# Weight decoding in one run of 24 steps, and the bias laid into the mixing's bank by ScalarE

## The chip, the core and the metric

The kernel runs on one core of a Trainium2 chip. Five engines work side by side, each through its own list of instructions in order: TensorE (PE; its weight loads are shown apart as PEld) multiplies matrices into PSUM banks, VectorE (DVE) and ScalarE (ACT) do elementwise work, GpSimd (POOL) does almost nothing here, and SyncE (SP) issues every DMA of the kernel. An instruction that needs another engine's result waits on a semaphore, and everything behind it on its engine waits too. The metric is device time in microseconds, the median of several runs. Before the change it is 1982.3 us (3 runs, 1982.04 to 1982.46).

## The reference, cut to what matters

```python
X = np.fft.rfft(x, axis=1)                      # x: 4 x 3072 x 256, along 3072
Yr = Xr @ w_r - Xi @ w_i + b_r                  # the mixing, 256 x 256
Yi = Xr @ w_i + Xi @ w_r + b_i
Yr = np.sign(Yr) * np.maximum(np.abs(Yr) - lam, 0.0)   # the same for Yi
x = np.fft.irfft(Yr + 1j * Yi, n=3072, axis=1)
h = x @ w_in;  g = h * np.tanh(softplus(h));  x = g @ w_out          # 256 -> 2048 -> 256
xk = mu_k * x + (1 - mu_k) * x_prev;  xr = mu_r * x + (1 - mu_r) * x_prev
k = np.maximum(xk @ w_k, 0);  out = sigmoid(xr @ w_r2) * (k * k @ w_v)   # 256 -> 1024 -> 256
```

All arrays are float32 but the weights of the last two layers, which the kernel reads as 64-bit words (`raw`, two int32 each) and decodes on the chip: float64 to a pair of float32r numbers, a high and a low part. Every product with such a pair is three matmuls.

## The kernel before

The kernel has two parts. `part1` does the two Fourier transforms with the mixing between them, `part2` the rest. Part 1 takes about 325 us, part 2 the other 1650 us, in which nothing is changed.

Part 1 splits the transform of 3072 into 24 x 128. The 24-point stage is additions on DVE (`f1_ops` forward, on a batch in a tile `a`; `f3_ops` inverse, on a tile `g`), the 128-point stage is matmuls. It runs 48 steps, u = 0 to 47: four batches (b) of 12 frequency groups (t, with `NT = 12`). For each u there are three pieces of PE work: F(u) (`emit_F`, eight records into a bank `xps`), M(u) (`emit_M`, the mixing into a bank `yps`, 12 matmuls and a 13th for the bias), I(u) (`emit_I`, into `bps`). Step u issues, in this order on PE, F(u+1), M(u), I(u-1). Between them stand ACT and DVE: `post_F` copies `xps` into `xh` (ACT) and the rest into `xl` (DVE), which M needs; `post_M` and `post_M2` are the shrinking of Y, `yb<-yps` once on ACT and once on DVE, which I needs; `post_I` copies `bps` into `bs` (ACT), which SP writes to DRAM (`b_dr`).

The bias goes in through PE: `pick` (a 128 x 128 selection of rows) times `bias` (b_r and b_i in two rows, as high and low part). In groups with t = 0 M consists of two halves of 256 columns with 13 matmuls each.

The engines' lists are laid down by the loop over u (`manual_schedule`): the text's order is each engine's order. DVE's additions are a background (`Background`) that the loop fills in between by a plan of costs: `bg.until` puts in additions up to a planned time, `bg.flush` all that fall due. `F1_AT` says when the forward additions of the next batch join it, `F3_PART1` when the two halves (h = 0, 1) of batch 0's inverse do; `bg.step` loads such a half (`g<-b_dr`, 1536 KB) as soon as the half before is through the list.

The decoding is a pipeline over pieces (`Weights`): `wq.vec()` lays down one piece's DVE work (`q<-raw` twice, `q<-q,sg`, and a subtraction of the piece two calls older), `wq.sca()` its ACT work (`sg`, `sg`, `q`, and the high part), and asks for the next piece's `raw` (512 KB). There are 25 pieces: 9 of w_k, w_v and w_r (`park_piece`, parked in DRAM as `w_dr`), 8 of w_in (`win_piece`) and 8 of w_out (`wout_piece`). Before the change five parked pieces are decoded in steps 6 to 14, one a step (`NPARK`, `PARK_AT`), and the other twenty in steps 36 to 47, two a step (`dec = 2`). In a step with `dec` the first `wq.vec()` stands ahead of `post_M2(u - 1)` and `post_F(u + 1)` on DVE:

```python
emit_F(u + 1); post_M(u - 1)
if dec: emit(wq.vec())
bg.until(...); post_M2(u - 1)
bg.until(...); post_F(u + 1)
if dec: emit(wq.sca(2))
post_I(u - 2)
if dec == 2: emit(wq.vec()); emit(wq.sca(2))
emit_M(u); emit_I(u - 1)
```

A batch of x is 3 MB in ten DMAs on SP (`new_a`, `load_x`), issued at t = 11 two batches ahead: at u = 11 and at u = 23. All DMAs are on SP's one queue.

Of the kernel before, what the change touches and what calls it, by code (L numbers as in the profile page):

```python
# [10 lines left out]
F32 = mybir.dt.float32  # L11
# [13 lines left out]
NB = 4  # L25
# [4 lines left out]
NT = 12  # L30
# [6 lines left out]
START = (20500, 20500)  # L37
SLACK = (2000, 3200)

NPARK = 5  # L40
PARK_AT = (6, 15)

F3_PART1 = {(1, 4): [(0, 0)], (1, 8): [(0, 1)]}
F3_PART2 = {1: (1, 0), 3: (1, 1), 5: (2, 0), 8: (2, 1), 10: (3, 0), 14: (3, 1)}
# [69 lines left out]
def tile_fft_mix_moe_channel_mix(  # L114
# [26 lines left out]
    def emit(ops):  # L141
        for e in ops:
            e()
# [10 lines left out]
    def mm(o, l, r, start, stop, **kw):  # L154
        T.matmul(out=o, lhsT=l, rhs=r, start=start, stop=stop, **kw)  # L155
# [258 lines left out]
    wt = {}  # L414
# [31 lines left out]
    def decode(raw, parts, scale=1.0):  # L446
        hw, lw = raw[:, :, 1], raw[:, :, 0]
        tl = {}

        def a0():  # L450
            sg = tl["sg"] = pools["st"].tile([128, 512], F32, tag="sg", name="sg")
            return [lambda: act(sg.bitcast(I32), hw.bitcast(F32), ACTF.Copy, scale=14000.0),
                    lambda: act(sg, sg.bitcast(I32), ACTF.Sign)]

        def v0():
            q = tl["q"] = pools["st"].tile([128, 512], F32, tag="q", name="q", bufs=3)
            qi = q.bitcast(I32)
            return [lambda: V.tensor_scalar(out=qi, in0=hw, scalar1=0x08000000, scalar2=3,
                                            op0=ALU.bitwise_xor, op1=ALU.logical_shift_left),
                    lambda: stt(qi, lw, 29, qi, ALU.logical_shift_right, ALU.bitwise_or)]  # L460

        def a1():
            return [lambda: act(tl["q"], tl["q"], ACTF.Abs)]

        def v1():
            return [lambda: stt(tl["q"], tl["q"], 3.4e38, tl["sg"], ALU.min, MULT)]

        def a2():
            tl["p"] = parts(tl["q"])
            return [lambda hi=hi, v=v: act(hi, v, ACTF.Copy, scale=scale) for hi, lo, v in tl["p"]]  # L470

        def v2():
            if scale == 1.0:
                return [lambda hi=hi, lo=lo, v=v: tt(lo, v, hi.bitcast(F32), SUB) for hi, lo, v in tl["p"]]
            return [lambda hi=hi, lo=lo, v=v: stt(lo, v, scale, hi.bitcast(F32), MULT, SUB)
                    for hi, lo, v in tl["p"]]

        return a0, v0, v1, a2, v2, a1

    def win_piece(i):  # L480
        raw = raw_piece(w_in[:, 256 * i:256 * i + 256])
        cs = slice(256 * i, 256 * i + 256)
        w = wt["in"]
        return decode(raw, lambda q: [(w[:, 0, :, cs], w[:, 1, :, cs],
                                q.rearrange("p (k f) -> p k f", k=2))])

    def wout_piece(i):
# [12 lines left out]
    def park_piece(i):  # L500
        raw = raw_piece(parked[i])
        tl = {}

        def parts(q):
            t = tl["t"] = yhl_p.tile([128, 2, 512], F32R, tag="yl", name="wp")
            return [(t[:, 0, :], t[:, 1, :], q)]
        a0, v0, v1, a2, v2, a1 = decode(raw, parts)
        return a0, v0, v1, a2, lambda: v2() + [lambda: nc.sync.dma_start(out=w_dr[i], in_=tl["t"].bitcast(F32))], a1
# [62 lines left out]
    def part1():  # L571
        with ExitStack() as es:
# [11 lines left out]
            fm, im = {}, {}  # L584
            bias = c1.tile([128, 512], F32R, name="bias")
            pick = c1.tile([128, 2, 128], F32R, name="pick")
            zero = c1.tile([128, 64], F32, name="zero")
            As = {}

# [25 lines left out]
            def post_F(u):  # L615
# [7 lines left out]
                if t == 0:  # L623
# [5 lines left out]
                                     in_=zero[:, 0:4].rearrange("p (a o) -> p a o", o=1), func=ACTF.Copy)  # L629
                    xt[u] += (zh, zl)  # L630

            def emit_M(u):
                t = u % NT
                ps = psy.tile([128, 512], F32, tag="y", name="yps")
                xs = xt.pop(u)
                if t:
                    groups = [(slice(0, 512), ((0, 256, 0), (1, 0, 0)))]
                else:

                    groups = [(slice(0, 256), ((0, 256, 0), (1, 0, 2))),  # L640
                              (slice(256, 512), ((0, 512, 2), (1, 256, 0)))]
                for gs, parts in groups:
                    n = gs.stop - gs.start
                    todo = []
                    for zl, lo in ((0, 0), (0, 1), (1, 0)):
                        for h in range(2):
                            w = wt["mix", h][lo]
                            for r, c0, z in parts:
                                todo.append((xs[z + zl][:, h, 128 * r:128 * r + 128], w[:, c0:c0 + n]))
                    todo.append((pick[:, 0 if t else 1, :], bias[:, gs]))  # L650
                    for i, (l, r) in enumerate(todo):
                        mm(ps[:, gs], l, r, i == 0, i == len(todo) - 1)
                yps[u] = ps


            def post_M(u):
                yb = yb_p.tile([128, 512], F32, tag="yb", name="yb")
                act(yb, yps[u], ACTF.Relu, bias=-LAM)
                ybt[u] = yb
# [66 lines left out]
            bg.add(both(z[8:], m[:4]) + m[4:])  # L726
            bg.flush()
            emit_F(0)
            post_F(0)
            bg.add(both(t0[0][1], t0[1][1]) + both(t0[0][2][:10], t0[1][2][:10]), 4)  # L730
            bg.add(both(t0[0][2][10:], t0[1][2][10:]), 8)
# [4 lines left out]
            for u in range(NU):  # L736
                b, t = divmod(u, NT)
                if t == NT - 1 and b + 2 < NB:
                    new_a(b + 2)
                if t == F1_AT[b] and b + 1 < NB:  # L740
                    hs = [f1_ops(As[b + 1], h) for h in range(2)]
                    for i, due in ((slice(14), 0), (slice(14, 24), 4), (slice(24, None), 8)):
                        bg.add(both(*[(h[0] + h[1])[i] for h in hs]), NT * (b + 1) + due)
                bg.jobs += F3_PART1.get((b, t), [])
                bg.step()
                if u == NU - NT - 1:
                    wt["in"] = big.tile([128, 2, 2, 2048], F32R, tag="big", name="win")
                    todo = [lambda: win_piece(0)]
                    for i in range(8):
                        if i < 7:  # L750
                            todo.append(lambda i=i: win_piece(i + 1))
                        todo.append(lambda i=i: wout_piece(i))
                    late = [lambda i=i: park_piece(i) for i in range(NPARK, 9)]
                    wq = Weights(todo[:6] + late + todo[6:])
                    wq.load(3)
                dec = 0
                if b == NB - 1:
                    dec = 2
                elif PARK_AT[0] <= u < PARK_AT[1]:
                    dec = 1  # L760
                    if u == PARK_AT[0]:
                        wq = Weights([lambda i=i: park_piece(i) for i in range(NPARK)])
                        wq.load(2)
                bg.flush(u + 1)
                if u == 6:
                    S.activation(out=mu1, in_=mu, func=ACTF.Copy, scale=-1.0, bias=1.0)
                pe += 1710 * (u + 1 < NU)
                if u + 1 < NU:
                    emit_F(u + 1)
                if u:  # L770
                    post_M(u - 1)
                if dec:
                    emit(wq.vec())
                    bg.clock += 2100
                if u:
                    bg.until(y_at + SLACK[0])
                    post_M2(u - 1)
                    y_at = bg.spend(y_at, 602)
                if u + 1 < NU:
                    bg.until(pe + 700 + SLACK[1])  # L780
                    post_F(u + 1)
                    x_next = bg.spend(pe + 700, 602)
                if dec:
                    emit(wq.sca(2))
                if u > 1:
                    post_I(u - 2)
                if dec == 2:
                    emit(wq.vec())
                    emit(wq.sca(2))
                    bg.clock += 2100  # L790
                emit_M(u)
                pe = max(pe, x_at + 300) + 2770
                y_new = pe + 700
                if u:
                    emit_I(u - 1)
                    pe = max(pe, y_at + 300) + 1710
                x_at, y_at = x_next, y_new
                if b == NB - 1 and t == 10:
                    bg.drain()
                    load_y(0)  # L800
            while wq.busy():
                emit(wq.vec())
                emit(wq.sca(2))
            for h in range(2):
                emit(split_y(0, h)[1])
            post_M(NU - 1)
            post_M2(NU - 1)
            post_I(NU - 2)
            emit_I(NU - 1)
            post_I(NU - 1)  # L810
# [256 lines left out]
```

## Time and profile before

| | |
|---|---|
| median of 3 runs | 1982.3 us (1982.04 to 1982.46) |
| the profiled execution's own time | 1981.86 us |
| its span (first to last instruction) | 1979.9 us |
| PE busy | 1958.0 us, 99% |
| DVE busy | 1141.4 us, 58% |
| ACT busy | 929.0 us, 47% |
| DMA | 106.66 MB, mean 54 GB/s |

The numbers of the trace are from one execution; times in it count from the span's start. An instruction's busy time reaches past the start of the next one on its engine, so what one costs its engine is read from start to start. The chain of waits follows back from the last instruction what released each: what stands in it set the time.

### The profile page before, as it was taken

The numbers are of one execution on the slowest core, as the hardware profiler recorded it, in microseconds if no ns is written. First come the engines' busy times: TensorE is split into PE (matmuls) and PEld (weight loads), VectorE is DVE, ScalarE is ACT, GpSimd is POOL, SyncE is SP. The second block draws the span as 40 slices with busy tenths as digits, with TensorE's granted clock in tenths as the row PEclk, the third lists the DMA queues.
The fourth block names the chain that finished last, engine by engine and source line by source line (L and its number), as shares of the span: only waits on it lengthen the run. The fifth ranks groups of instructions, "written<-read, shape, count | busy, mean of one in ns | idle before, by whom it ended". The sixth has DMA issues, their size and how long they took to land.

```text
span 1979.9 us, 25685 instructions
## 1 busy us (share of the span) xinstructions
PE 1958.0 (99%) x10084; PEld 1686.2 (85%) x10084; DVE 1141.4 (58%) x2183; ACT 929.0 (47%) x1525; POOL 13.2 (1%) x28
## 2 busy tenths in 40 slices
PE   6999999999999999999999999999999999999999
PEld 5888888888888888888888888888888888888888
DVE  8999976665654754465375445555544544444444
ACT  2422286344544554454445444444544544454455
POOL 0000000000000000000000000000000000000000
PEclk9999999999999999999999999999999999999999
DMA  9445276111011010101101001011000000000000
GB/s 279 150 138 170 70 245 200 39 32 65 22 33 54 22 44 11 54 22 33 54 22 54 1 22 54 5 33 38 22 1 22 22 11 12 22 23 1 22 11 22
DMA packets 104554, 106.66 MB, mean 54 GB/s; under 512 B 7017, under 2 KB 85489, under 8 KB 103409
## 3 DMA queue, kind: packets, MB, share of 16 engines
q1 hardware_dynamic: 104432, 105.02, 16.7%
q8 instruction: 79, 1.29, 0.3%
q14 instruction: 43, 0.34, 0.1%
HBM read 62.53 MB, written 42.47 MB: 53 GB/s over the span
## 4 chain that ended last, share of the span: by engine, by line
PE 97%; DMA 1%; DVE 1%; ACT 0%; issue 0%; SPq 0%; DVEq 0%; ACTq 0%
PE a L155 26%; PE hps L155 26%; PE v L155 14%; PE kps L155 13%; PE yps L155 7%; PE bps L155 4%; PE xps L155 4%; PE zps L155 3%; DMA a<-in_x_dram 1%; DMA w_dr<-wp 0%; DVE g L146 0%; ACT sg L152 0%; SPq L266 0%; DVE q L149 0%; ACT q L152 0%
## 5 line engine op out<-in xcount | busy, mean ns | idle before, releaser
L863 DVE CAST gh<-u 128x512 fp32r<-128x512 f32 x384 | 163.2, 425 | 747.5 <-PE a L155 598.2
L155 PE MATMUL a<-gh,wo 128*128 128x512 f32 x1536 | 536.3, 390 | 0.0
L155 PE MATMUL hps<-yh,win 128*128 128x512 f32 x1536 | 534.7, 389 | 0.0
L152 ACT ACTIVATE u<-hps 128x512 f32<-128x512 f32 x384 | 229.7, 598 | 525.0 <-PE hps L155 368.8
L155 PEld LDWEIGHTS hps<-yh,win 128*128 128x128 f32 x1536 | 288.3, 188 | 60.3
L155 PEld LDWEIGHTS a<-gh,wo 128*128 128x128 f32 x1536 | 288.4, 188 | 58.0
L155 PE MATMUL a<-gl,wo 128*128 128x512 f32 x768 | 299.9, 390 | 0.0
L155 PE MATMUL hps<-yl,win 128*128 128x512 f32 x768 | 298.8, 389 | 0.0
L155 PE MATMUL kps<-b,wkt 128*128 128x512 f32 x960 | 280.1, 390 | 0.0
L155 PE MATMUL v<-b,kh 128*128 128x256 f32 x1536 | 275.8, 281 | 0.0
L146 DVE TENSOR_TENSOR gl<-u,gh 128x512 fp32r<-128x512 f32 x384 | 263.6, 687 | 3.6
L155 PEld LDWEIGHTS v<-b,kh 128*128 128x128 f32 x1536 | 243.7, 190 | 7.6
L155 PE MATMUL v<-b,kl 128*128 128x256 f32 x768 | 215.8, 281 | 0.0
L155 PEld LDWEIGHTS kps<-b,wkt 128*128 128x128 f32 x960 | 179.1, 188 | 36.1
L152 ACT ACTIVATE ka<-kps 128x512 f32<-128x512 f32 x192 | 115.0, 599 | 185.5 <-PE kps L155 185.5
L155 PEld LDWEIGHTS hps<-yl,win 128*128 128x128 f32 x768 | 144.1, 188 | 29.9
L155 PEld LDWEIGHTS a<-gl,wo 128*128 128x128 f32 x768 | 144.5, 188 | 26.6
L146 DVE TENSOR_TENSOR kl<-ka,kh 128x512 fp32r<-128x512 f32 x192 | 132.5, 690 | 32.8 <-ACT ka L152 19.1
L155 PEld LDWEIGHTS v<-b,kl 128*128 128x128 f32 x768 | 144.1, 188 | 0.0
L152 ACT ACTIVATE ka<-ka 128x512 f32<-128x512 f32 x192 | 121.4, 632 | 6.3
L152 ACT ACTIVATE kh<-ka 128x512 fp32r<-128x512 f32 x192 | 121.4, 632 | 6.3
L146 DVE TENSOR_TENSOR g<-g 128x128 f32<-128x128 f32 (+3 forms) x272 | 107.5, 433 | 1.2
(80 smaller groups left out, 1926.8 us busy)
## 6 DMA issues: line engine op xcount, KB each, us to landing
b_dr<-bs SPq DMA_DIRECT2D x48, 256.0 KB, 2.2
g<-b_dr SPq DMA_DIRECT2D x8, 1536.0 KB, 6.8
y<-y_dr SPq DMA_DIRECT2D x48, 256.0 KB, 3.2
out_dram<-r SPq DMA_DIRECT2D x48, 256.0 KB, 2.2
y_dr<-g SPq DMA_DIRECT2D x80, 64.0 KB, 1.6
w_dr<-wp SPq DMA_DIRECT2D x9, 512.0 KB, 5.9
a<-in_x_dram SPq DMA_DIRECT2D x8, 512.0 KB, 6.2
y_dr<-g SPq DMA_DIRECT2D x32, 128.0 KB, 1.9
```

The lines of the kernel that those rows point to most:

```text
L146: V.tensor_tensor(out=o, in0=a, in1=b, op=op)
L152: S.activation(out=o, in_=i, func=f, **kw)
L155: T.matmul(out=o, lhsT=l, rhs=r, start=start, stop=stop, **kw)
L863: return [lambda: V.tensor_copy(hi, u), lambda: tt(lo, u, hi.bitcast(F32), SUB)]
```

## The change

It does two things, and three small ones go with them.

The decoding: all 25 pieces are one pipeline, begun at the end of step 23's preparations (`DECODE_FROM = 24`) and run one piece a step in steps 24 to 47, two in steps 38, 41, 43 and 45 (`TWICE`). The nine parked pieces come first. At most two `raw` tiles are asked for ahead, where it was three.

The bias: the two possible bias images (all rows alike; the first row different, for t = 0) are made once by two matmuls `cps<-bias,pick`, and ACT copies them into SBUF (`full`). For u of 3 and more, `pre_M(u)` has ACT copy `full` into the bank `yps`, a step ahead of M(u), and all of M's matmuls add to it (`start` is False). For u below 3 `pre_M` is still a matmul. Of 52 bias matmuls (44 of 512 columns, 8 of 256) five remain, of 512 columns.

Beside these, the plan's cost of M is lowered from 2770 to 2550, the bank `yps` of u+1 is taken in step u rather than in step u+1, and at the end of part 1 the shrinking of the last Y stands ahead of the splitting of part 2's first input on DVE.

```diff
-NPARK = 5
-PARK_AT = (6, 15)
+DECODE_FROM = 24
+TWICE = (38, 41, 43, 45)
...
+            full = [c1.tile([128, 512], F32, name=f"full{i}") for i in range(2)]
...
+            def pre_M(u):
+                ps = yps[u] = psy.tile([128, 512], F32, tag="y", name="yps")
+                i = 0 if u % NT else 1
+                if u < 3:
+                    mm(ps, pick[:, i, :], bias, True, False, skip_group_check=True)
+                else:
+                    act(ps, full[i], ACTF.Copy)
+
             def emit_M(u):
...
-                ps = psy.tile([128, 512], F32, tag="y", name="yps")
+                ps = yps[u]
...
-                    todo.append((pick[:, 0 if t else 1, :], bias[:, gs]))
                     for i, (l, r) in enumerate(todo):
-                        mm(ps[:, gs], l, r, i == 0, i == len(todo) - 1)
-                yps[u] = ps
+                        mm(ps[:, gs], l, r, False, i == len(todo) - 1, skip_group_check=True)
...
             emit_F(0)
+
+            for i in range(2):
+                ps = psb.tile([128, 512], F32, tag="b", name="cps")
+                mm(ps, pick[:, i, :], bias, True, True)
+                act(full[i], ps, ACTF.Copy)
             post_F(0)
...
-                    todo = [lambda: win_piece(0)]
+                if u == DECODE_FROM - 1:
+                    todo = [lambda i=i: park_piece(i) for i in range(9)] + [lambda: win_piece(0)]
...
-                    late = [lambda i=i: park_piece(i) for i in range(NPARK, 9)]
-                    wq = Weights(todo[:6] + late + todo[6:])
-                    wq.load(3)
-                dec = 0
-                if b == NB - 1:
-                    dec = 2
-                elif PARK_AT[0] <= u < PARK_AT[1]:
-                    dec = 1
-                    if u == PARK_AT[0]:
-                        wq = Weights([lambda i=i: park_piece(i) for i in range(NPARK)])
-                        wq.load(2)
+                    wq = Weights(todo)
+                    wq.load(2)
+                dec = 0 if u < DECODE_FROM else 2 if u in TWICE else 1
...
+                if u == 0:
+                    pre_M(0)
+                if u + 1 < NU:
+                    pre_M(u + 1)
...
-                pe = max(pe, x_at + 300) + 2770
+                pe = max(pe, x_at + 300) + 2550
...
+            post_M(NU - 1)
+            post_M2(NU - 1)
             for h in range(2):
                 emit(split_y(0, h)[1])
-            post_M(NU - 1)
-            post_M2(NU - 1)
```

Since the freed steps 6 to 14 let the background run earlier, the change moves work that its lines do not name. The first place is SP's list around the load of the fourth batch of x (`a<-in_x_dram`, step 23). Before, the stores of the first inverse half (`y_dr<-g`) stand behind it:

```order
L266 DMA a<-in_x_dram 128x5x128
L266 DMA a<-in_x_dram 128x8x128
L291 DMA y_dr_70<-g 128x3x128
L291 DMA y_dr_70<-g 128x128
L678 DMA b_dr_58<-bs 128x2x256
L291 DMA y_dr_70<-g 128x2x128
```

and in the changed kernel all sixteen stores of that half stand ahead of the ten pieces of x (the last eleven between two `b_dr` stores directly ahead of x), and behind x the load of the second half and two loads of `raw`:

```order
L266 DMA a<-in_x_dram 128x5x128
L266 DMA a<-in_x_dram 128x8x128
L277 DMA g<-b_dr_57 128x3072
L442 DMA raw<-in_moe_w_k_dram 128x2x512 x2
L685 DMA b_dr_58<-bs 128x2x256
L442 DMA raw<-in_moe_w_k_dram 128x2x512
```

What moved: the stores from behind x to ahead of it, and 1536 KB of `g` and 512 KB for each `raw` to directly behind it. The second place is DVE's list at step 24. Before, yb(23) stands between the additions of the inverse half:

```order
L146 TENSOR_TENSOR xl<-xps,xh 128x512
L146 TENSOR_TENSOR g<-g 128x512
L149 SCALAR_TENSOR_TENSOR yb<-yps,yb 128x512
L149 SCALAR_TENSOR_TENSOR g<-g 128x4x128 x2
L149 SCALAR_TENSOR_TENSOR g<-g 128x512 x2
L149 SCALAR_TENSOR_TENSOR g<-g 128x4x128 x2
L146 TENSOR_TENSOR xl<-xps,xh 128x512
```

and in the changed kernel those additions are through, and the first piece's two instructions stand between xl(24) and yb(23):

```order
L149 SCALAR_TENSOR_TENSOR g<-g 128x4x128 x2
L146 TENSOR_TENSOR xl<-xps,xh 128x512
L149 SCALAR_TENSOR_TENSOR yb<-yps,yb 128x512
L146 TENSOR_TENSOR xl<-xps,xh 128x512
L458 TENSOR_SCALAR q<-raw 128x512
L149 SCALAR_TENSOR_TENSOR q<-raw,q 128x512
L149 SCALAR_TENSOR_TENSOR yb<-yps,yb 128x512
L146 TENSOR_TENSOR xl<-xps,xh 128x512
```

What moved: yb(23) now stands behind an instruction that reads the first `raw`. The third place is DVE's list from one yb to the next where two pieces are decoded. Before (such a step in the last batch; DVE has only the two pieces and `xl`):

```order
L149 SCALAR_TENSOR_TENSOR yb<-yps,yb 128x512
L146 TENSOR_TENSOR xl<-xps,xh 128x512
L146 TENSOR_TENSOR wp<-q,wp 128x512
L149 SCALAR_TENSOR_TENSOR q<-q,sg 128x512
L458 TENSOR_SCALAR q<-raw 128x512
L149 SCALAR_TENSOR_TENSOR q<-raw,q 128x512
L146 TENSOR_TENSOR wp<-q,wp 128x512
L149 SCALAR_TENSOR_TENSOR q<-q,sg 128x512
L458 TENSOR_SCALAR q<-raw 128x512
L149 SCALAR_TENSOR_TENSOR q<-raw,q 128x512
L149 SCALAR_TENSOR_TENSOR yb<-yps,yb 128x512
```

and in the changed kernel, from step 38 to step 39 (the second inverse half's additions on `g` stand there too):

```order
L146 TENSOR_TENSOR g<-g 128x256 x2
L146 TENSOR_TENSOR g<-g 128x128 x7
L146 TENSOR_TENSOR xl<-xps,xh 128x512
L146 TENSOR_TENSOR win<-q,win 128x2x256
L149 SCALAR_TENSOR_TENSOR q<-q,sg 128x512
L458 TENSOR_SCALAR q<-raw 128x512
L149 SCALAR_TENSOR_TENSOR q<-raw,q 128x512
L146 TENSOR_TENSOR wo<-q,wo 128x256 x2
L149 SCALAR_TENSOR_TENSOR q<-q,sg 128x512
L458 TENSOR_SCALAR q<-raw 128x512
L149 SCALAR_TENSOR_TENSOR q<-raw,q 128x512
L149 SCALAR_TENSOR_TENSOR yb<-yps,yb 128x512
```

What moved: additions on `g`, which before were done ahead of the last batch, stand in the same stretch as two pieces.

## Rows read from the trace of the kernel before

**Rows 1.** The page: granted clock by slice, and the chain's shares by engine.

```profile
PEclk9999999999999999999999999999999999999999
...
PE 97%; DMA 1%; DVE 1%; ACT 0%; issue 0%; SPq 0%; DVEq 0%; ACTq 0%
```

**Rows 2.** The longest wait of PE in part 1: us in total, times, longest.

```profile
PE xps L155 <- DVE g L146: 17.6, 2, 16.2
```

**Rows 3.** The chain, in order of time: start, us, records.

```profile
19.19 4.84 PE xps L155 x12
...
35.61 2.96 PE yps L155 x13
...
167.96 0.89 PE xps L155 x8
...
178.38 1.73 PE bps L155 x8
```

**Rows 4.** Timeline of PE, a bias matmul and what follows: start, us.

```profile
108.08 0.39 PE L155 MATMUL yps<-bias,pick 128*128 128x512 f32 x1
108.31 1.90 PE L155 MATMUL bps<-im,yb 128*128 128x256 f32 x8
```

**Rows 5.** Timeline of SP's issues, steps 23 and 24 and the start of step 36.

```profile
164.89 9.18 SPq L266 DMA_DIRECT2D a<-in_x_dram  x10
...
171.69 2.37 SPq L266 DMA_DIRECT2D a<-in_x_dram  x1
...
177.01 7.30 SPq L291 DMA_DIRECT2D y_dr<-g  x14
...
246.01 1.01 SPq L442 DMA_DIRECT2D raw<-in_moe_w_in_dram  x2
```

**Rows 6.** DMAs, us to landing: step 23's last x; w_dr behind x; all w_dr.

```profile
a<-in_x_dram SPq DMA_DIRECT2D x1, 512.0 KB, 7.7
...
w_dr<-wp SPq DMA_DIRECT2D x1, 512.0 KB, 6.5
...
DMA to landing us min/median/max: 2.6/5.9/6.5
```

**Rows 7.** Stretches: us; PE, PEld, DVE, ACT, POOL busy (x); clock; DMA; GB/s.

```profile
187.50:190.50 3.00, 3.00 (x15) 2.52 (x14) 3.00 (x4) 1.09 (x2) 0.00 (x0) 1.00 0.97 348
...
186.00:248.00 62.00, 62.00 (x286) 53.00 (x285) 57.56 (x131) 17.82 (x33) 0.00 (x0) 1.00 0.31 96
248.00:318.00 70.00, 69.74 (x328) 59.78 (x327) 59.24 (x107) 62.09 (x119) 0.00 (x0) 1.00 0.68 220
```

**Rows 8.** The same stretch, DVE's instructions on the decoding's tile q alone.

```profile
248.00:318.00 70.00, 46.61 (x85) 1.00 0.68 220
```

**Rows 9.** Timeline of DVE: a first piece, and a step with two pieces.

```profile
250.13 0.43 DVE L458 TENSOR_SCALAR q<-raw 128x512 int32<-128x512 int32 x1 [3.60 <-DMA raw<-in_moe_w_in_dram]
...
251.20 0.69 DVE L149 SCALAR_TENSOR_TENSOR yb<-yps,yb 128x512 f32<-128x512 f32 x1
...
272.66 0.68 DVE L146 TENSOR_TENSOR xl<-xps,xh 128x512 fp32r<-128x512 f32 x1
...
276.79 0.69 DVE L149 SCALAR_TENSOR_TENSOR q<-q,sg 128x512 f32<-128x512 f32 x1 [0.40 <-ACT q L152]
...
278.46 0.68 DVE L149 SCALAR_TENSOR_TENSOR yb<-yps,yb 128x512 f32<-128x512 f32 x1
```

**Rows 10.** Timeline of DVE: small additions, back to back.

```profile
213.80 1.42 DVE L146 TENSOR_TENSOR a<-a 128x256 f32<-128x256 f32 x4
215.14 1.69 DVE L149 SCALAR_TENSOR_TENSOR a<-a 128x128 f32<-128x128 f32 x8
```

**Rows 11.** Timeline of weight loads at the start of the program.

```profile
23.40 0.34 PEld L155 LDWEIGHTS yps<-wmh,xh 128*128 128x128 f32 x1
...
24.57 0.19 PEld L155 LDWEIGHTS yps<-wml,zh 128*128 128x128 f32 x1
```

**Rows 12.** Timeline of ACT: the first zl, and what it waits for.

```profile
24.21 0.63 ACT L627 ACTIVATE zl<-xl 128x512 fp32r<-128x512 f32 x1 [2.14 <-DVE xl L146]
```

More of the change, by code (lines that the diff above doesn't have):

```diff
@@ L482, in win_piece @@
         cs = slice(256 * i, 256 * i + 256)
-        w = wt["in"]
-        return decode(raw, lambda q: [(w[:, 0, :, cs], w[:, 1, :, cs],
+        return decode(raw, lambda q: [(wt["in"][:, 0, :, cs], wt["in"][:, 1, :, cs],
                                 q.rearrange("p (k f) -> p k f", k=2))])
```

## The prediction

> **What bounds the kernel now.** I read the chain of waits first: PE holds 97% of it [rows 1]. Then PE's own waits in part 1: the long one is 17.6 us at the program's start, until DVE has the first additions [rows 2]. From there the chain goes from one PE piece to the next: a mixing with 13 matmuls takes 2.96 us, eight records of 256 columns 1.73 [rows 3], so that a step of F, M and I is 1.73 + 2.96 + 1.73 = 6.42 us of PE, 48 times, without a hole. What PE no longer does is gained in full, and whatever makes PE wait is lost in full. So the question is not whether a bias matmul is worth something, but whether DVE, ACT and SP keep up with a PE that is faster by a bias matmul a step, while the decoding lies on them at another place.
>
> **The bias matmuls.** From the start of one to the next instruction's is 108.31 - 108.08 = 0.23 us [rows 4]; 2.96 / 13 is 0.228. M(3) to M(47) lose one each (two halves in groups with t = 0): 45 x 0.228 = **-10.3 us**. A step becomes 6.19 us. Two matmuls for `full` and two of `pre_M` come ahead of M(0), in the slow start where twelve records took 4.84 us, 0.4 each [rows 3]: at most 4 x 0.4 = 1.6, at least nothing, since M(0) waits there for `zl` anyway, which stood at 24.21 behind `xl` [rows 12]. I take **+0.8**.
>
> **What ACT takes over.** One copy of 512 a step, some 0.5 us, a step ahead of its M. ACT was busy 17.8 us of 62 in steps 25 to 35 and 62.1 of 70 in 36 to 47 [rows 7]; there it loses seven of twenty pieces and gains twelve copies, so it gets emptier. The copy waits until DVE has read the bank (yb(u-2), a step earlier); behind it on ACT stand yb(u-1) and xh(u+1). DVE is done with that yb before M(u) can start at all, so this wait adds nothing of its own: 0; without that cover it would be 0.5 a step. The new order at the end of part 1 is covered by the last two I, 2 x 1.73 us [rows 3], against a yb and a split of some 1.8 us on DVE: 0.
>
> **What moves on SP.** With no decoding in steps 6 to 14, DVE gets to the first inverse half of batch 0 earlier. Two things follow in SP's list at step 23: that half's stores stand ahead of the fourth batch of x, and since the half is through, the next one's load (`g`, 1536 KB) is laid down at once, between x and the first `raw`. And on DVE yb(23) stands behind the two instructions that read that `raw`. I(23) needs yb(23). So I follow this transfer, in the clock of the trace before:
>
> - F(24) starts at 167.96, I(23) is due at 178.38, 10.4 later [rows 3]; less two bias matmuls, 9.95 after F(24).
> - x is issued from 164.89 [rows 5], 3.1 ahead of F(24). Now eleven stores stand ahead; fourteen took 7.30 us of SP [rows 5], so eleven take 5.7. They wait for the half's last additions, in step 22. I put x 4 us later, 0.9 after F(24); bounds are 3.1 ahead and 2.6 after.
> - The last x was issued at 171.69 and landed 7.7 us later [rows 5, 6], at 179.4: 14.5 after the first issue.
> - `g` then moves 1.57 MB; at the 348 GB/s of its load before [rows 7] that is 4.5 us, and the first `raw`, 0.52 MB, at the same rate 1.5. It lands 20.5 us after the first issue, 21.4 after F(24).
> - DVE needs 251.20 - 250.13 + 0.69 = 1.8 us from the first piece's start to the end of yb [rows 9]: 23.2 after F(24).
>
> PE waits 23.2 - 9.95 = **+13.2 us**. That transfers queue up so is seen at step 11: a store issued directly behind x landed after 6.5 us, where the fastest took 2.6 [rows 6]. If x is not delayed, it is 9.2; if it is delayed by all stores, 14.9.
>
> **What the wait does to PE's clock.** After its idle time at the start, PE's weight loads took 0.34 us, and 0.19 from 24.57 on [rows 11]. The twelve records from 19.19 took 4.84 us [rows 3]; eight of 256 columns at 1.73 and four of 128 at 0.11 are 2.2: 2.6 us dearer, a part of it small waits for DVE. The page's granted clock stands at 9 in every slice, that one too [rows 1], so it does not show this. A wait of 13 us in the middle may cost as much again: 0 to 2.6, and I take **+2**. The Trainium skill (TensorE: Matmul & The Clock Gate, Part 1: The HAM clock gate) says that the array is gated to 1.2 GHz when it has stood idle and goes back to 2.4 GHz only under sustained work; by that rule some 2 are due; by the granted clock of the profile's page nothing is, and the sum would be 2 lower.
>
> **What moves on DVE.** Its instructions on q are 46.61 us for twenty pieces [rows 8], 2.33 a piece. In 186 to 318 DVE was busy 57.56 + 59.24 = 116.8 us of 132 [rows 7], the second inverse half included. Five more pieces come into these steps: 128.5. And the 132 us shrink by 20.6 steps x 0.23 to 127.3. DVE is overbooked even without a wait. Where it shows: in the steps with two pieces. Before, from `xl` at 272.66 to yb at 278.46 are 5.8 us, yb is 0.6, together a whole step of 6.4 with nothing else on DVE, and 0.4 of it a wait for ACT's q [rows 9]. In steps 38, 41 and 43 additions on `g` stand there too: in step 38 two of 256 and eight of 128 columns, at 1.42 / 4 = 0.35 and 1.69 / 8 = 0.21 [rows 10]: 2.4 us. 6.4 + 2.4 less the 0.4 that DVE then comes late to anyway is 8.4 against 6.2: 2.2 over. By step 45 the half is through. Three times 2.2, with what the single steps between give back and a late ACT takes again: 6.5. At the first step of the last batch ACT's chain of `zh` and `zl`, which waited 2.14 us for `xl` at the start [rows 12], stands ahead of a piece whose low part DVE waits for: some 2.5 more. Together **+9**; 4 if the single steps win back what the double ones lose, 12 if each of the four steps loses 3.
>
> **The sum.** -10.3 + 0.8 + 13.2 + 2 + 9 = +14.7. On the profiled execution's own 1981.86 (span 1979.9) that is 1996.6; the median of the runs is 0.4 above it, 1982.3, so 1997 for it. Part 2 is PE from end to end and gets the same inputs in the same order: 0. The ends: -10.3 + 0 + 9.2 + 0 + 4 = +2.9 (1985) and -10.3 + 1.6 + 14.9 + 2.6 + 12 = +20.8 (2003).
>
> **Rivals.**
>
> *The late steps absorb the overload* (chance 0.15). DVE's lead and the single steps cover the three double ones. For it: before, two pieces a step for twelve steps cost PE next to nothing. Against: DVE then had no additions. -10.3 + 0.8 + 13.2 + 2 + 1 = +6.7: 1989.
>
> *The first piece arrives early* (0.10). Decides at step 24: if the queue serves `raw` beside x and `g` and not behind them, `raw` is issued when SP is through with ten x in 9.18 us [rows 5], and lands 250.13 - 246.01 = 4.1 later [rows 5, 9], 13.3 after the first issue. With x undelayed the wait is 13.3 - 3.1 + 1.8 - 9.95 = 2.1, and PE's clock stays. -10.3 + 0.8 + 2.1 + 9 = +1.6: 1984, not slower within what can be told. Against it stands the store behind x [rows 6].
>
> *Both* (0.05): -10.3 + 0.8 + 2.1 + 1 = -6.4: 1976, faster.
>
> **How the numbers follow.** My forecast, a wait of 11 to 15 at step 24 and 6 to 12 in the late steps, has 0.70 and lies in 1990 to 2002. About 0.2% (4 us) is what a measurement of this kernel can tell from no change. Slower by more: 0.70 + 0.15, and a little of the early piece, 0.86. Within: the rest of that rival, 0.08. Faster: 0.06. The range 1987 to 2002 leaves out the two rivals with an early piece and the far tail.
>
> **What would show it.** Among PE's waits a single one of 11 to 15 us, for DVE's yb, some 10 us after F(24); DVE there idle for `raw` of w_k some 20 us; weight loads of 0.34 us right after. Between about 260 and 325 us four waits of PE of 2 to 3 us for yb, in the first step of the last batch and the steps with two pieces. `yps` pieces of the chain at 2.73 us with 12 records. If PE waits less than 5 us at step 24, the transfers are wrong; if the late waits are missing, the load on DVE is. If the mixing pieces are not 0.23 shorter, the saving is.

## The result, and the profile after

| | before | after |
|---|---|---|
| median of the runs, us | 1982.17 | 2000.22 |
| the runs, us | 1981.73 to 1982.46 | 1996.28 to 2002.45 |
| profiled execution, us (span) | 1981.86 (1979.9) | 2002.44 (2000.4) |
| ratio to before, 95% interval | | 1.0086, 1.0072 to 1.0100 |

The changed kernel is slower by 0.86%; predicted were 1997 us and slower. One of its six runs took 2457 us and is left out of the range and the ratio, though not of the median; the median of the other five is 1998.0.

First the page of the kernel after: PE's row and the granted clock by slice, then the chain's shares by engine.

```profile
PE   6996998999999999999999999999999999999999
...
PEclk9998999999999999999999999999999999999999
...
PE 88%; DVE 7%; DMA 2%; SPq 1%; issue 1%; ACT 0%; DVEq 0%; ACTq 0%
```

Before, PE held 97% of the chain and the clock stood at 9 throughout [rows 1]; now DVE, DMA and SP hold a tenth, and the fourth slice (150 to 200 us) has a gap and a lower clock. The waits of PE after 30 us, where before has a single one of 0.3 us, and those of DVE for `raw` after 160 us (us in total, times, longest):

```profile
PE bps L155 <- DVE yb L149: 24.0, 5, 15.3
...
DVE q L458 <- DMA raw<-in_moe_w_k_dram: 21.1, 1, 21.1
...
DVE q L458 <- DMA raw<-in_moe_w_out_dram: 3.6, 1, 3.6
...
DVE q L458 <- DMA raw<-in_moe_w_in_dram: 2.0, 1, 2.0
```

All of PE's waits are for `yb`, one of them of 15.3 us; DVE is late with that `yb` because it stands 21.1 us for the first `raw` of w_k. The chain around it (start, us, what), which answers to the predicted queue on SP:

```profile
157.52 2.42 DVE g L149 x4
159.94 0.23 SPq L291
...
164.70 0.41 SPq L266
...
168.85 4.74 SPq L266
...
175.81 1.62 SPq L277
177.47 9.21 DMA raw<-in_moe_w_k_dram
186.70 0.44 DVE q L458
187.16 0.69 DVE q L149
187.86 0.61 DVE yb L149
188.51 3.78 PE bps L155 x8
192.30 2.73 PE xps L155 x8
```

DVE's last additions of the first half end at 159.94; then come the stores (L291), the ten loads of x (L266), `g` (L277) and `raw`, and only behind the two instructions on q the `yb` that I(23) needs. The last two rows are PE pieces that take 1.73 each undisturbed [rows 3]: together 3.05 us longer. The granted clock was low over them (stretch: length, PE busy, granted clock, DMA share, GB/s):

```profile
187.00:188.50 1.50, 0.00 (x0) 0.50 0.95 362
188.50:195.00 6.50, 6.49 (x17) 0.56 0.43 130
195.00:230.00 35.00, 35.00 (x160) 1.00 0.52 173
318.00:324.00 6.00, 3.08 (x14) 0.99 0.85 247
324.00:330.00 6.00, 5.46 (x13) 0.50 0.14 48
```

It is at 0.50, the lower of its two levels (1.2 GHz), when the wait ends, and at 1.00 (2.4 GHz) again from 195. The same happens once more at 324, around the end of a wait of 3.5 us. A mixing has the twelve records that were predicted, at 2.73 us (the chain, start and us), for 2.96 with thirteen [rows 3]:

```profile
201.23 2.73 PE yps L155 x12
```

The late waits stand in this part of the chain:

```profile
301.01 0.17 SPq L291
...
302.22 4.32 DMA raw<-in_moe_w_in_dram
...
306.63 0.44 DVE q L458
...
312.44 2.40 DVE g L149 x4
...
316.73 0.26 SPq L291
...
318.50 4.14 DMA raw<-in_moe_w_out_dram
...
322.73 0.44 DVE q L458
...
324.54 3.78 PE bps L155 x8
328.32 2.98 PE xps L155 x8
```

Both times stores of `g` (L291) stand on SP directly ahead of a `raw` that DVE then waits for. The account goes by the distance from one I to the next, read from the starts of the `bps` pieces of both traces (47 of them, since the last two I follow each other directly). Undisturbed it is 6.41 us before and 6.19 after; near the groups with t = 0 it differs a little, after for example 6.33 at I(11), I(23) and I(35) and 6.22 at I(12), I(24) and I(36):

| place | us over the undisturbed distance |
|---|---|
| I(23), wait for `yb` behind `raw` | 15.45 |
| I(24), low clock | 2.88 |
| I(35) to I(37), first step of the last batch | 0.75 |
| I(38), behind double step 38 | 2.01 |
| I(41), behind double step 41 | 3.42 |
| I(43), behind double step 43 | 3.62 |
| I(44), low clock | 3.16 |
| I(39), I(42) | 0.22 |
| sum | 31.5 |

Less 10.3 for the bias matmuls and 0.6 that before lost in its late steps, this is +20.6: the spans differ by 2000.4 - 1979.9 = 20.5. Part 2 (from the first `hps` on) begins at 347.8 instead of 327.2, and it lasts 1652.6 us in both.

### The profile page after: what moved, and what is told of

Read it like the earlier page. It is cut to its first block, busy times and chain, and to the rows that moved or that the text cites. A ratio compares the mean times of both kernels' runs of the same rounds, so it can differ in the third digit from the quotient of the medians.

```text
span 2000.4 us, 25607 instructions
## 1 busy us (share of the span) xinstructions
PE 1955.1 (98%) x10037; PEld 1681.7 (84%) x10037; DVE 1140.1 (57%) x2183; ACT 951.5 (48%) x1572; POOL 12.7 (1%) x28
## 4 chain that ended last, share of the span: by engine, by line
PE 88%; DVE 7%; DMA 2%; SPq 1%; issue 1%; ACT 0%; DVEq 0%; ACTq 0%
PE a L155 26%; PE hps L155 26%; PE v L155 13%; PE kps L155 13%; PE zps L155 3%; PE yps L155 3%; PE bps L155 2%; PE xps L155 2%; DVE a L146 1%; DVE g L146 1%; SPq L266 1%; DVE a L149 1%; DVE q L149 1%; DMA a<-in_x_dram 1%; DVE yb L149 1%; DVE xl L146 1%
## 5 line engine op out<-in xcount | busy, mean ns | idle before, releaser
L155 PE MATMUL bps<-im,yb 128*128 128x256 f32 x384 | 94.8, 391 | 24.0 <-DVE yb L149 24.0
```

## The experiments

The twelve kernels ran four at a time on one chip beside the kernel before, whose medians there were 1981.9, 1982.0 and 1982.8. What a distance between two I loses is counted as in the table above.

**The bias change alone**, on the kernel before, with its decoding where it was:

```
+            def pre_M(u):
...
+                    act(ps, full[i], ACTF.Copy)
...
-                    todo.append((pick[:, 0 if t else 1, :], bias[:, gs]))
...
-                pe = max(pe, x_at + 300) + 2770
+                pe = max(pe, x_at + 300) + 2550
```

> The kernel before with the bias change alone: no bias matmul from M(3) on, ScalarE's copies of `full` in their place, the decoding where it was (five pieces in steps 6 to 14, twenty in the last batch). Theory A (the saving stands by itself): 45 x 0.228 = 10.3 us less, some 1972 to 1973. Theory B (the last batch of before had no room to spare: two pieces a step kept DVE and ACT busy for a whole step of 6.42 us of PE): where PE needs only 6.19, DVE sets the step, so in steps 36 to 47 nothing is gained or PE waits 1 to 2 us in each of several steps, and with another wait at step 11 the saving is mostly gone: -5 to +4, 1977 to 1986. In A PE has no new wait for yb; in B several between 260 and 330 us.

Measured: 1992.4, +10.4 (ratio 1.0053, 1.0038 to 1.0068), beyond even theory B. Up to I(11) the saving is there; then 1.7 us go at I(12), 9.3 from I(37) to I(46), and 6.1 in a wait at the end, with a low clock behind it. PE's waits after 30 us, and two places of the chain:

```profile
PE bps L155 <- DVE yb L149: 14.3, 8, 6.1
```

```profile
305.71 0.61 DVE g L146
306.33 0.36 SPq L291
...
307.75 4.08 DMA raw<-in_moe_w_out_dram
...
311.91 0.44 DVE q L458
...
324.55 0.16 SPq L291
...
327.37 3.51 DMA y<-y_dr
...
332.06 0.61 DVE yb L149
...
332.71 3.78 PE bps L155 x8
```

Additions on `g` stand beside two pieces a step, where before has none after 245 us, and they bring stores that `raw` and then part 2's first `y` wait behind. The planner, told of 2550 ns, gives each step less time for additions, and what it left over fell into the last batch; the sixth run tests this.

**The decoding moved alone**: the changed kernel with the matmul back in M and 2770.

> The changed kernel with the bias matmuls back in M: the decoding moved alone. If the two parts add up, it is slower than the changed kernel by the 10.3 us of the matmuls: some 2009 to 2012, +27 to +29 over before, with the wait at step 24 about the 15 us that the changed kernel shows. Rival: PE's longer steps give DVE and the transfers back what the matmuls cost, as the late waits and the wait at step 24 shrink by some tenths of a us a step: +18 to +22, 2000 to 2004, no dearer than the changed kernel.

Measured: 2002.6 (1.0106, 1.0091 to 1.0121): the rival. On top of the moved decoding the bias change is worth 2 us by the medians and 4 by the ratios, not 10. PE's waits after 30 us, the longest at I(23):

```profile
PE bps L155 <- DVE yb L149: 14.1, 3, 9.6
```

Here DVE had `raw` at 186.01, against 186.70 in the changed kernel: nearly the same time, though PE came to I(23) at 178.2 and not at 173.2. What 22 mixings saved, 22 x 0.228 = 5.0, PE for the most part waited for instead: the two runs below that have the changed kernel's program up to there, but for one more `raw`, wait 13.2, the ninth 13.7, so that some 4 of the 5.0 went into the wait; the profiled 15.3 has 1.6 to 2.1 more of its own.

**The first raw loaded earlier**: `if u == DECODE_FROM - 1` becomes `- 4`, so the load comes at step 20, the decoding stays.

> The changed kernel with one thing moved: the first two pieces of raw are loaded at step 20, ahead of the 3 MB of x and of g on SP's queue; they are decoded from step 24 on as in the changed kernel. Theory (raw stands behind x and g): the wait of 15 us at step 24 shrinks to 0 to 4 us (the third piece still stands behind x), and the granted clock does not fall there: 14 to 18 us less than the changed kernel, some 1981 to 1985. Rival (the wait is DVE's own load, or g and x hold PE by another way): less than 5 us won, 1992 or more.

Measured: 1986.4 (1.0028, 1.0016 to 1.0039), 13.8 below the changed kernel's median and 11.6 below that of its five runs, so a little less than the 14 to 18 of the theory. At I(23) and I(24) nothing is left; the third piece, issued behind x and `g`, costs 1.8 us at I(25). The late steps remain, with a low clock behind a wait of 3.4 at I(41). The first step of the last batch now loses more than in the changed kernel, 2.2 at I(35) and 1.8 at I(36) instead of 0.4 and 0.2.

**g behind raw**: `bg.step()` moved below `wq.load(2)`.

> The changed kernel with one thing moved: the 1536 KB load of g for the second inverse half is issued behind the first two raw, not ahead of them; x stays ahead. Theory (the queue serves in the order of issue): raw lands earlier by the time that g takes, 4.5 us, and the wait at step 24 falls from 15.4 to about 11, the clock loss behind it stays: some 4 to 5 us less than the changed kernel, 1992 to 1998. Rival (transfers in flight share the engines, so it matters little which is issued first): less than 1.5 us won.

Measured: 1995.1 (1.0066, 1.0051 to 1.0081). In its chain `raw` follows x directly and DVE has it at 181.90, 16.9 us after x's first issue, where the changed kernel took 22.0 and the runs with `g` ahead took 19.8 to 21.0:

```profile
172.31 2.48 SPq L266
174.83 7.04 DMA raw<-in_moe_w_k_dram
...
183.06 0.61 DVE yb L149
183.71 3.78 PE bps L155 x8
```

The wait is 9.9. Moving `g` behind `raw` brought `raw` forward by 2.9 to 5.1 us, so here what was issued first was also served first, as the theory had it, and x alone costs the larger part of the wait.

**raw three deep**: `wq.load(2)` and `wq.sca(2)` become 3.

> The changed kernel with raw prefetched three deep, not two, from the first load on; the decoding stays where it is. Theory (in the late steps q waits for a raw that was issued too late, behind the stores of y_dr on SP): the waits of PE in steps 41 and 43 (3.3 and 3.5 us, and 3.2 for the clock behind the second) shrink to 0 to 2 each and the clock stays up; the wait at step 24 stays (15 us): 4 to 8 less than the changed kernel, 1991 to 1996. Rival (the additions on g fill DVE in the double steps, and raw is late only because DVE frees it late): less than 2 us won.

Measured: 1991.6 (1.0049, 1.0035 to 1.0063), 8.6 below the changed kernel's median, inside the range of the theory. I(41) is 1.33 late instead of 3.42, I(43) not at all, and the clock behind it stays up; I(38) keeps its 2.01. The wait at I(23) is 13.2 here, since DVE had `raw` 20.2 us after x's first issue. The program up to there is the same but for one more `raw` at the end: the issue that held SP for 4.74 us held it for 2.81.

**The bias change alone, planner at 2770.**

> The bias change alone, as in the first run, with one number put back: the planner counts 2770 ns for a mixing and not 2550, so that DVE's additions stand in the same steps as in the kernel before. Theory C (the loss of the first run came from additions on g that the shorter count pushed out of steps 13 to 35 into the last batch, beside two pieces a step): the waits of 1.5 us in steps 38 to 44 and the wait of 6 us at the end go, one of 1.7 at step 12 stays, the single steps lose some tenths: 7 to 10 less than before, 1972 to 1975. Rival D (ScalarE's copies, which wait for the bank, or the shorter step itself hold the last batch): the waits stay, 1985 or more.

Measured: 1980.9 (0.9994, 0.9985 to 1.0003), so the saving is still missing. (The profiled execution, 1983.4, is the slowest of the eleven; its I(0) starts at 33.9, not at 32.0.) Theory C holds for the additions: after 245 us none on `g` is left, the wait at the end is gone, and what I(33) to I(45) lose is 5.1, not 9.3. But the wait at I(12) is 2.85, and the clock falls behind it:

```profile
101.27 6.26 DMA w_dr<-wp
...
107.55 0.63 ACT wp L152
108.18 0.49 ACT bs L152
108.66 0.49 ACT yps L152
109.16 0.52 ACT yb L152
...
109.70 0.70 DVE yb L149
...
110.45 2.95 PE bps L155 x8
```

A store of w_dr behind x, as long as before [rows 6], holds ACT's next `wp`, and behind that the copy into the bank and `yb`. Counted from I(0), PE comes here eleven mixings, 11 x 0.228 = 2.5 us, sooner than before. A copy of ScalarE lies on the path here, 0.49 us, and rival D holds for a part of the last batch: from 291.71 to 318.12 the chain stays on ACT, which with two pieces a step and a copy takes 6.6 us from one copy to the next, where PE needs 6.19:

```profile
298.30 0.49 ACT yps L152
...
304.89 0.49 ACT yps L152
```

So beside two pieces in every step the copy is not free: I(42) to I(44) lose 0.4 each.

**Both changes to raw**: loaded at step 20, three deep.

> The changed kernel with both: the first raw loaded at step 20, and three deep throughout. Theory (both waits come from SP's one queue): no wait over 1 us at steps 24 to 26, the late waits 0 to 2 each, no fall of the clock: 3 to 9 below the run with raw early alone (1986.4), 1977 to 1983. Rival (what is left there is DVE's load): 1984 or more.

Measured: 1978.4 (0.9981, 0.9972 to 0.9990), inside the range of the theory. What is left is 2.2 and 1.8 at I(35) and I(36), 0.6 at I(38), 1.4 at I(41). The theory's "no fall of the clock" failed: the 1.8 is a fall to 0.50 behind the wait of 1.98 at I(35), and the third run's 1.8 there is the same.

**The decoding spread out**: raw three deep, first loaded at step 5, and

```
-DECODE_FROM = 24
-TWICE = (38, 41, 43, 45)
+DECODE = (6, 8, 10, 12, 14, 16, 18, 20, 22, 24, 26, 35, 36, 37, 38, 39, 40, 41, 42, 43, 44, 45, 46, 47)
+TWICE = (40, 42, 44, 46)
```

> The changed kernel with its decoding placed anew: the first eleven steps of decoding in every second step from 6 to 26 and none from 27 to 34, so that the second inverse half's additions are through before the last batch; double steps at 40, 42, 44 and 46; raw three deep, first loaded at step 5. Theory (all of the loss is where the decoding stands): no wait over 3 us, no fall of the clock, the late steps lose 1 to 5 in all: 4 to 9 below the kernel before, 1973 to 1978. Rival (two pieces in a step of 6.19 us cost PE 2 us or more whatever else stands there): 1980 to 1986.

Measured: 1974.0 (0.9962, 0.9949 to 0.9974). One wait is left, 2.4 us at I(40).

**The planner's count in the changed kernel**: 2550 back to 2770.

> The changed kernel with one number put back: the planner counts 2770 ns for a mixing and not 2550. It tells why the changed kernel's wait at step 24 (15.4 us) is longer than that of the decoding alone (9.6), which has the bias matmuls and 2770. Theory P (DVE is busy without a hole from 111 to 161 us, so the first half's stores, x, g and raw come at a fixed time; a PE that is faster by 0.228 a step only comes to I(23) earlier and waits for longer): the wait stays at 13 to 15.5 us, 1996 to 2003. Theory Q (the shorter count put the additions later, and with them the chain of transfers): the wait falls to 9 to 11 us, some 5 less than the changed kernel, and the late waits may change by 2 either way: 1992 to 1997.

Measured: 2001.3 (1.0094, 1.0080 to 1.0108), theory P. The wait at I(23) is 13.7, so it is not the count that made it longer than 9.6. DVE's stretches in the changed kernel (length, busy, granted clock, DMA share, GB/s) show why the transfers come at a fixed time:

```profile
111.00:137.00 26.00, 26.00 (x69) 1.00 0.32 112
137.00:161.00 24.00, 23.73 (x53) 1.00 0.23 69
161.00:186.00 25.00, 1.51 (x3) 0.82 0.87 262
```

From 111 to 161 DVE has next to no hole (0.3 of 50 us): the first half's last addition ends when DVE is through, however early PE is.

**The second half's additions left out** but for its first two, raw three deep; its loads and stores stay.

> The run with raw three deep, with the second inverse half's additions left out after the first two (its loads and stores stay, so the output lacks that half). Theory (what that run still loses in the last batch, 2.0 us at step 38 and 1.3 at 41, is the additions on g beside two pieces in a step): PE has no wait over 0.5 us in steps 37 to 46, some 3.5 to 4 us less than that run: 1987 to 1989. Rival (two pieces in a step cost that by themselves): the waits at 38 and 41 stay, less than 1.5 won. The wait of 0.4 at step 35 (zh and zl) stays in both.

Measured: 1988.2 (1.0028, 1.0017 to 1.0038), 3.5 below the run with them. From I(38) to I(45) every distance is 6.19: with `raw` three deep two pieces in one of several steps cost PE nothing, and the additions were the rest. I(35) to I(37) keep 0.75.

**Spread out, double steps at the end**: `TWICE = (43, 44, 45, 46)`.

> The run with the decoding spread over steps 6 to 26, with its double steps moved from 40, 42, 44 and 46 to 43, 44, 45 and 46, behind the last additions on the fourth batch of x (due by step 44) and on g. Theory: the one wait that was left there (2.4 us, step 40) goes, and PE has no wait over 0.5 us behind the start of the program: 2 to 3 less than that run, 1971 to 1972, the whole 10.3 of the bias matmuls below before. Rival (four double steps in a row outrun raw, as in the last batch of the bias change alone): waits of 1.5 us in steps 44 to 46, and nothing won: 1974 or more.

Measured: 1971.45 (0.9946, 0.9933 to 0.9958), faster than both kernels. PE has no wait for `yb` left that makes a row; I(39) to I(41) lose 0.5 together.

**The same with the matmuls back** (2550 kept, so that DVE's order is the same).

> The same placing of the decoding with the bias matmuls back in M and ScalarE's copies taken out. Theory (where nothing makes PE wait, the matmuls cost what they take): 45 x 0.228 = 10.3 us more than with the copies, 1981 to 1983, no different from before. Rival (the copies cost something on ScalarE, or the new placing gains or loses something of its own): less than 8 or over 12 between the two.

Measured: 1981.7 (0.9996, 0.9986 to 1.0005): 1981.73 - 1971.45 = 10.28 between the two.

## Why the prediction was right, point by point

- **What bounds it.** "What PE no longer does is gained in full, and whatever makes PE wait is lost in full": yes, and both ends were run, 10.28 us of saving against 31.5 us of loss. (The long wait at the start is 16.2 us; the 17.6 read there is two waits together [rows 2].)
- **The bias matmuls, -10.3.** 10.28 where nothing makes PE wait. The +0.8 for the early ones can't be told: I(0) began at 32.0 before and 32.1 after, but between 31.9 and 34.7 in the other runs.
- **ScalarE's copies and the new end, 0.** The saving with the copies is the whole of the matmuls in the last two runs, so they cost nothing there. My cover fails where ACT itself is late: 0.49 us at I(12) in the sixth run, and 0.4 a step in its last batch, with two pieces in every step. The changed kernel's chain has no copy on it after 30 us. The order at the end wasn't tried by itself.
- **The wait at step 24, +13.2 (9.2 to 14.9).** The mechanism was right in each link: stores, x, `g`, `raw`, q, `yb`. The size is 15.3 in the profiled execution, 13.2 in two runs that are alike up to there and 13.7 with the planner's other count. Two terms were short. x was first issued 1.6 after F(24) (164.70 and 163.10), not 0.9. And DVE had `raw` 22.0 after that issue where I had 20.5: x and `g` held SP until 177.47, with 4.74 us in a single issue of x, and `g` landed 19.9 after the first issue where my terms give 19.0. How long the last x took to land no row shows, and that the one long issue made the difference is not shown. The 4.5 for `g` fits: with `g` behind, `raw` came 5.1 sooner than in the profiled execution and 3.3 sooner than with `raw` three deep.
- **What I did not see in it.** I placed x by PE's clock (0.9 after F(24)). It goes by DVE's, which has next to no hole for 50 us ahead of it. So the wait contains most of what PE had saved until then. The sum was not touched, since I counted the whole saving and the whole wait, but that the decoding alone costs 13.2 + 2 + 9 = +24 would have followed from my terms, and it costs 20.6.
- **The clock, +2 (0 to 2.6).** 2.88 behind the long wait, 1.9 to 2.8 in the other runs that have it. The Trainium skill (TensorE: Matmul & The Clock Gate, Part 1: The HAM clock gate) says that an idle array is gated to 1.2 GHz. Here the profile's granted clock agrees: 0.50. The 9 that the page shows at the program's start did not speak against it: the first clock record of that trace begins at 24.41 us, where the weight loads become shorter [rows 11], and time without a record counts as full. The second fall, 3.16 at I(44), I had not counted.
- **The late steps, +9 (4 to 12).** 10.0 without the clock's 3.2, but not from where I had it. Step 38 went as worked out, 2.0 for my 2.2, with additions on `g` as the excess. The `zh` and `zl` chain at the first step was sized at 2.5 and cost 0.75. In the third and seventh run, where PE does not wait at I(23), it costs 2.2 and a fall of the clock 1.8 more; that the long wait covers it in the changed kernel is likely but was not tested by itself. At I(41) and I(43) additions were not the larger part: with `raw` three deep 2.1 and 3.6 of their 3.4 and 3.6 went, and the low clock too. So the additions cost 3.5 (by the tenth run), and `raw` behind stores cost 5.7, with 3.1 more for the clock. I had followed the queue on SP for step 24 and not for the stores that the same additions issue in steps 40 to 43. What I gave the additions and `zh` too much and what I left out nearly cancel, so that 10.0 comes so near to 9 is luck.
- **The rivals.** The early piece fell with `raw` at 22.0 us, the late steps that absorb with 10.0.
- **The sum.** Against +20.5 in the profiled execution, +14.7 is 5.8 short. The parts make 6.0: 2.2 in the wait, 0.9 in the clock behind it, 1.0 in the late steps and 3.2 in the second fall, less 0.7 for the early matmuls, which do not show, and 0.6 that before lost in its late steps. That 1997 is so near to 1998.0, the median of the five runs, is partly luck: it rests on the three faster ones, whose terms no trace shows.

Open stays why two runs of the changed kernel took 2002.4 and three 1996.3 to 1998.0. The profiled one is of the former; its wait at I(23) is 2.1 longer than in the runs alike and its second fall of the clock cost 3.2, together about the 5 us that lie between. That the three faster ones lack both is a guess; they left no trace.

## What to carry to other kernels

Work that is paced by another engine or by a queue does not come earlier because the bound engine got faster: here some 4 of the 5.0 us saved up to such a point were waited away at it, so look for the first of them. When loads are moved, list what stands ahead of them on the queue that issues them, stores that other work brings along included, and issue the small, urgent one before the big one. A planner's constant that is brought up to date moves work too. And what costs nothing on an engine with room costs its full time where that engine sets the step, as the copy does in the sixth run's last batch.

## What was not expected of the hardware

The granted clock fell to 0.50 behind short waits as well as long ones: behind 3.5 us at I(43) in the changed kernel, not behind 3.3 at I(41) of the same execution; at I(12) of the sixth run behind 2.85 (0.66 over the piece that follows); and at I(35) of the seventh behind 1.98 (0.61 from 250.2 to 253). It did not fall behind 2.39 at I(40) of the eighth run or 2.68 at I(38) of the ninth, nor behind the waits of 1.1 to 1.6 us in the first. So the length of the wait alone does not decide it. The price was 1.7 to 3.2 us each time, for the short ones nearly as much as the wait itself.

The seventh load of x in step 23 held SP for 4.74 us in the changed kernel, 2.81 with `raw` three deep, 3.36 without the additions and 1.42 with `g` behind `raw`, though the program up to there is the same; what decides that, no run here shows.
